# A new written order for TensorE's instructions in a fused attention and gated feed-forward kernel

## The chip, the cores and the metric

The kernel runs on one core of one Trainium2 chip. The metric is device time in microseconds (us). It is the median of several runs; beside it stands one profiled execution with its trace. A core has TensorE (PE, matrix products; PEld is its weight load), VectorE (DVE), ScalarE (ACT), GpSimd (POOL) and SyncE (SP), which run side by side and wait for each other by semaphores. TensorE writes into PSUM, a small memory of eight banks, from which VectorE and ScalarE read.

## The reference

The input x has 4 batches of 12,416 tokens with 128 features. Two attention steps go through 32 inducing points, and a gated feed-forward layer of width 1,536 follows. The types are float32 outside; the kernel computes in float16 with float32 sums.

```python
def mab(q, kv):                       # softmax attention, kv is key and value
    s = scale * (q @ kv.transpose(0, 2, 1))
    s = s - s.max(-1, keepdims=True)
    a = np.exp(s)
    a /= a.sum(-1, keepdims=True) + 1e-09
    return a @ kv
h = mab(I, x)                         # I: the 32 inducing points; h: 32 x 128 per batch
y = mab(x, h)                         # 12,416 x 128 per batch
gate = 1.0 / (1.0 + np.exp(-(y @ w_gate)))
out = (gate * (y @ w_val)) @ w_out    # width 1,536 in between
```

## The kernel before

**Stages.** The first attention (stage 1: h from x) of batch 0 is a prologue of about 30 us. The second attention's weights (stage 2) and the feed-forward layer then run as one long main stretch, in which stage 1 of the next batch is worked in. Since y = a2 @ h, the kernel multiplies h with both feed-forward weights once per batch (`hw`), so the hidden layer is a product of the 32 attention weights a2 with `hw`: a matrix product whose contraction is only 32 long.

**Blocks and chunks.** The tokens lie in 97 blocks of 512 (4 columns of 128). The hidden width of 1,536 is cut in 12 slices of 128. A *chunk* is one slice for one block: a 128 x 512 tile of the hidden layer. Nine chunks of the last batch are worked out apart, by ScalarE and GpSimd (`plan_aside`, L1194); 1,155 remain, in one row. For each chunk there are four kinds of work:

- *Gate*: TensorE multiplies `hw`'s gate part by a2 (32*128 form, L1120, `g_ps`), then ScalarE takes a tanh (L1163) into a ring of 16 chunks in SBUF (`t`). Gates go in units of 2 and 1 chunks in turn, each with a PSUM tile of its own.
- *Value*: TensorE multiplies `hw`'s value part by a2 (same form, same line 1120) into one of two places in PSUM: `v_ps` (two banks) or `vm_ps` (two banks, of which the second also serves the side tasks below).
- *Product*: VectorE forms u = (t + 1) * v (L1350) in one instruction, for one chunk (512 wide) or for two (1024 wide). This is nearly all that VectorE does in the main stretch.
- *Output*: TensorE multiplies u by w_out, four matmuls of the full 128*128 form a chunk (L1249, `acc_ps`). When a block's 48 are done, ScalarE evacuates the sum (L1274) and SyncE writes it out.

The 32*128 form uses a quarter of the array's rows. Row group 0 or 1 is a gate's, for an even or an odd slice, 2 or 3 a value's, and matmuls on different row groups run side by side. TensorE runs them in the order in which they are written.

**Products in pairs.** Products come in first and second ones by turns. A first product reads `v_ps` and takes two chunks. A second one reads `vm_ps`: one chunk (a `V` pair) or two (a `W` pair, only possible while no side task holds the second bank of `vm_ps`).

**Side tasks.** Stage 1 and stage 2 of later blocks and batches are chains of steps over TensorE, ScalarE, VectorE, GpSimd and the DMA queues (`plan_stage1`, `plan_stage2`, `plan_combine`, `plan_aside`). Each has a position, a chunk number from which it may be taken (`TIMES`, `ASIDE`); `turn_page` (L1305) looks for them at every first product. GpSimd's and the DMA steps are issued at once; those of TensorE, VectorE and ScalarE lie in lists until the written order calls them. The loads of x and its transposes are issued by `turn_page` too, at given chunk numbers.

**The written order.** `ORDER`, a string of letters at the top, says in which order instructions are issued; the last loop (L1400) carries it out letter by letter:

- `g`: the next gate unit (`issue_gate`, L1155): its matmuls and its tanh.
- `V` or `W`: the next value fill (`fill_value`, L1322). Of two in a row that form a pair, the first letter says whether the second product has one chunk (`V`) or two (`W`).
- `x`: the product of the fill before it (`product`, L1337).
- `oN`: the next N output matmuls, from a queue to which each product adds four a chunk.
- `p`, `a`, `d`: the next TensorE, ScalarE or VectorE step of a side task.

So a letter's place sets the order on every engine. Between engines nothing is fixed: each waits by semaphores for what it reads and for the buffers that it writes. The product's results have four buffers each for first and second products (L137). A wide product has a no-op ahead of it that waits for its tanhs.

Of the kernel before, what the change touches and what calls it, by code (L numbers as in the profile page):

```python
# [59 lines left out]
4Vxo4go8Vxa0go4pgVxo4pa0gWxo8gVxo8Wxgo8a0gVxgo16gVxgpVxpo4a0gWxo4Vxgo8go4gVxo8gVxo4pa0gVd0xa0gVx  # L60
o20gWxo4Vxgo8go4gVxo8pVxo4Vxa0gpVxgo12Vxa0ggVxo12gVxgo4gVxo4pgVd0xVxo4go12Vxa0a0ggVxo12Vxa0gpgVd
0xo12Vxgo8a0gVxo4VxgpVd0xgo12a0gVxgpVxo8pa0gVxo4pVxgpo4a0gWxo12gVxo4gVxo8gpVd0xgo8a1a0gWxgo8Vxo4
Wxgo8go4gVxo8gVxo8gpVxgpVxa0go8Vxa0gVxo4Vxgpgo8Vd0xVxgo24Vxa0ggVxo12a0gVxpa0gVxo12gVxo4pa0gVxo4p
gVxo12a0gVxo4gVxo4pgVxo8pa0a0gVd0xgVxo12pa0gWxo4gVxo8ggWxo8gVxo8gWxo8a1gVxgo8Vxgo8pVxgo4pVxa1go8
a0gVxo8gWxo8gVxo4a0gWxgo12Vxgo4gWxo8gVxgo8Vxgo8gVxo8a0gVxgo4Vxo8Vxa0go12gVxgVxo4Vxgpo4gVd0xo4gVd
0xo12Vxa0gpo4pVxa0go4gWxo4Vxgo8go4gWxo8gVxo8Vxgo8a0gpa0gVxo8Wxgo8gVxo8Wxgo4Vxgo4ggWxo8gVxo8a0gWx
go8gVxo8gWxo12Vxa0ggo8gVxo8po4a0a0gVxgWxo12Vxgo4Wxgo8gVxgo8gWxo8gVxo8a0ggWxo8gVxo8gVxo4go4pVxpa0
gWxgo12Vxgo8Wxgo4a0gVxgo8gWxo8gVxo8gWxo4go4gVxo8gWxo8a0gVxgo12Wxa0go4Vxgo8gWxo4ggVxo8gWxo12a0gVx
go12Wxgo4gVxo8gWxgo8gVxo4go12Vxa0gpVxgo4pVxa0go8Vxgo8Wxgo4Vxgo8gVxo4go4pVd0xgo8Vxa1a0go12Vxgo4Wx
go4Vxgo8Wxggo4Vxgo16Vxa0gVxgo8pVd0xgo16Vxa0gVxgppVxa0go8Wxgo4Vxgo12a0gWxgo4Vxgo8Vxa0go12ppa0gVxo  # L70
4Wxgo4gVxo8gWxo8a0gVxgo8Vxgo12pgVxo4pa0gVxo4Vxgo12gVxo8a0gVxpVd0xgo12a0gVxo4gWxo4Vxgo4go8Vxgo4Vx
go8Vxgo4a0gVxpVd0xgo4a0gVxo16WxggVxo12gVxgo8pVxgo4pVxo4a0a0gVxgo4Vxa0go12pVd0xgVxo12a0gVxgpo4Vd0
xo4Vxgo12Vxa0gpo4pa0gVxo4gVxpo4pVxa0go4gWxo8Vxgo8ggVxo4Vxgo4pVd0xgo8a1a0gVxgo8Wxo8Vxgo4Wxgo4ggVx
o12gVxo12Vxa0gpgo8Vd0xVxgo8a0go8Vxgo4pVxgo8Vxa0go4Vxgo8Vxa0gppVxa0go8Vxa0go4pVxpa0gWxgo12Vxgo8gV
# [24 lines left out]
o8a0gVxo4gVxpo8a0gVxo4gVxo16Vxa0gVxgo16gVxpa0gVxo16gVxo8Vxgo8Vxa0gVxgo12Vxgo4Vxgo8gVxo8Vxgo4gVxo
4Vxgo8a0gVxgo8VxgVxo4gVxo12VxpVxa0go12gVxgVxo8gVxo4a0gVxgo12VxVxo20Vxo16  # L100
"""


# [1339 lines left out]
```

## Time and profile before

| what | value |
| --- | --- |
| median of 3 runs | 726.4 us (724.94 to 727.75) |
| profiled execution, its own time | 723.66 us |
| its span, first to last instruction | 721.9 us |
| mean granted TensorE clock | 0.996 |
| busy: PE, DVE, ACT, POOL | 684.1, 701.4, 679.2, 445.9 us |
| the prologue, 0 to 30.6 us: DVE busy | 20.33 us |
| the main stretch, 50 to 710 us: PE, DVE, ACT busy | 632.90, 655.10, 640.67 us |

Rows of groups give line, engine, operation, what is written and read with shapes, count, then busy time and mean duration of one in ns, then the idle time ahead of them and what ended it. Rows of the timeline give start, duration, engine, line, operation and count, with the idle time ahead in brackets; several like instructions in a row are one row. Rows of waits give who waited for whom, the sum in us, how often, and the longest. Matmuls overlap and their ends are modelled, so TensorE's busy time says little of how full it is; starts are surer than ends.

### The profile page before, as it was taken

The page shows a single profiled execution, that of the slowest core. Times are in us where ns is not written, and L with a number is a line of the kernel's source. Part 1 is how long each engine was busy: PE and PEld are TensorE (multiplying, and loading weights), DVE is VectorE, ACT ScalarE, POOL GpSimd, SP SyncE. Part 2 cuts the span into 40 slices and gives each one's busy share as a digit, 9 for nine tenths or more (in the row PEclk, how much of TensorE's full clock was granted, in tenths as well). Part 3 has the DMA queues.
Part 4 walks back from the last instruction along what each step waited for, and adds up shares of the span by engine and source line. Part 5 has one row for each costly group of instructions (what it writes and reads, how often), then busy time and mean ns, then how long its engine had stood idle before and what let it go on. Part 6 is the DMA issues. An engine that isn't in the chain of part 4 may idle for free.

```text
span 721.9 us, 21194 instructions
## 1 busy us (share of the span) xinstructions
PE 684.1 (95%) x8446; PEld 401.4 (56%) x8446; DVE 701.4 (97%) x763; ACT 679.2 (94%) x1019; POOL 445.9 (62%) x718
## 2 busy tenths in 40 slices
PE   8899999999999999999999999999999999999997
PEld 4455555555555555555555555555555555555555
DVE  6899999999999999999999999999999999999997
ACT  4699999999999999999999999999999999999996
POOL 4464762888753747488666266378766768776220
PEclk9999999999999999999999999999999999999999
DMA  9799494244458273326178431321220221223111
GB/s 210 119 175 138 107 172 103 60 104 103 91 114 162 66 135 76 74 64 130 49 114 170 102 78 38 89 59 45 62 75 36 69 75 45 61 74 61 45 45 46
DMA packets 118179, 65.74 MB, mean 91 GB/s; under 512 B 101408, under 2 KB 102208, under 8 KB 118080
## 3 DMA queue, kind: packets, MB, share of 16 engines
q1 hardware_dynamic: 112176, 50.90, 30.7%
q0 software_dynamic: 5584, 13.34, 11.0%
q8 instruction: 66, 1.08, 0.6%
q14 instruction: 33, 0.27, 0.1%
q10 hardware_dynamic: 320, 0.15, 0.1%
HBM read 27.80 MB, written 25.43 MB: 74 GB/s over the span
## 4 chain that ended last, share of the span: by engine, by line
PE 52%; ACT 23%; DVE 10%; issue 9%; POOL 3%; DMA 2%; ACTq 0%; DVEq 0%; POOLq 0%
PE acc_ps L1249 25%; ACT t L1163 18%; PE g_ps L1120 13%; DVE u L1350 10%; PE v_ps L1120 5%; PE vm_ps L1120 4%; ACT o L1274 3%; DMA xn<-in_x_dram 2%; PE vm_ps L650 1%; PE vm_ps L427 1%; DMA a2r<-a2n 1%; ACT e L711 1%; ACT a1T L392 1%; POOL a2n L765 1%; PE vm_ps L367 0%
## 5 line engine op out<-in xcount | busy, mean ns | idle before, releaser
L1163 ACT ACTIVATE t<-g_ps 128x1024 f16<-128x1024 f32 (+1 forms) x770 | 588.4, 820 | 19.2 <-ACT t L1163 4.1
L1350 DVE SCALAR_TENSOR_TENSOR u<-t,v_ps 128x1024 f16<-128x1024 f16 (+1 forms) x332 | 401.4, 1209 | 4.1 <-PE v_ps L1120 1.2
L1249 PE MATMUL acc_ps<-wo,u 128*128 128x128 f16 x4596 | 364.2, 220 | 6.6 <-ACT o L1274 1.1
L1249 PEld LDWEIGHTS <-u 128*128 128x128 f16 x4620 | 265.2, 98 | 152.7 <-issue 145.1
L1350 DVE SCALAR_TENSOR_TENSOR u<-t,vm_ps 128x512 f16<-128x512 f16 (+1 forms) x330 | 311.9, 945 | 2.4 <-PE vm_ps L1120 0.9
L1120 PE MATMUL g_ps<-a2r,hwt 32*128 32x512 f16 (+1 forms) x1179 | 287.9, 375 | 13.8 <-ACT t L1163 6.9
L1120 PEld LDWEIGHTS <-hwt 32*128 32x128 f16 x2382 | 97.1, 91 | 128.2 <-issue 55.9
L1120 PE MATMUL v_ps<-a2r,hwt 32*128 32x512 f16 (+1 forms) x677 | 127.2, 374 | 6.4 <-DVE u L1350 4.6
L1120 PE MATMUL vm_ps<-a2r,hwt 32*128 32x512 f16 (+1 forms) x502 | 126.3, 377 | 1.2 <-DVE u L1350 0.9
L719 POOL TENSOR_TENSOR sum<-e 128x256 f32<-128x256 f16 (+1 forms) x23 | 15.4, 671 | 122.3 <-ACT e L711 119.4
L765 POOL TENSOR_TENSOR a2n<-e,rs 128x2048 f16<-128x2048 f16 (+3 forms) x25 | 86.8, 3474 | 3.7 <-DVE rs L737 1.9
L743 POOL TENSOR_TENSOR near<-sme,minus 128x16 f32<-128x16 f32 (+1 forms) x22 | 65.3, 2966 | 1.7
L1274 ACT ACTIVATE o<-acc_ps 128x512 f32<-128x512 f32 x96 | 57.9, 603 | 0.8 <-PE acc_ps L1249 0.4
L698 POOL TENSOR_SCALAR rise<-rise 128x256 f32<-128x256 f32 (+6 forms) x110 | 51.2, 465 | 9.7
L697 POOL TENSOR_TENSOR rise<-sc 128x256 f32<-128x256 f32 (+1 forms) x22 | 16.2, 739 | 32.6 <-ACT sc L687 32.5
L699 POOL TENSOR_TENSOR top<-top,rise 128x128 f32<-128x128 f32 (+3 forms) x88 | 28.4, 323 | 7.3
L719 POOL TENSOR_TENSOR sum<-sum 128x128 f32<-128x128 f32 (+3 forms) x92 | 28.4, 309 | 7.2
L697 POOL TENSOR_TENSOR rise<-top 128x128 f32<-128x128 f32 (+3 forms) x88 | 27.3, 310 | 6.9
L1214 POOL TENSOR_SCALAR xn_spare<-xn_spare 128x512 f32<-128x512 f16 x9 | 13.4, 1492 | 19.9 <-ACT xn_spare L1212 19.9
L702 POOL TENSOR_TENSOR sc<-sc,top 128x512 f32<-128x512 f32 (+1 forms) x22 | 23.9, 1086 | 1.7
L1219 POOL TENSOR_TENSOR xn_spare<-xn_spare 128x512 f16<-128x512 f32 x9 | 11.4, 1272 | 21.2 <-ACT xn_spare L1217 21.1
L650 PEld LDWEIGHTS <-xT 128*128 128x128 f16 x388 | 14.0, 96 | 7.2 <-issue 6.8
(165 smaller groups left out, 330.9 us busy)
## 6 DMA issues: line engine op xcount, KB each, us to landing
out_dram<-o SPq DMA_DIRECT2D x96, 256.0 KB, 2.1
xn<-in_x_dram POOLq DMA_DIRECT2D x18, 512.0 KB, 6.6
xn<-in_x_dram POOLq DMA_DIRECT2D x3, 544.0 KB, 8.2
xn<-in_x_dram POOLq DMA_DIRECT2D x3, 256.0 KB, 12.6
xn<-in_x_dram SPq DMA_DIRECT2D x1, 576.0 KB, 5.6
xn<-in_x_dram SPq DMA_DIRECT2D x1, 512.0 KB, 4.7
a2r<-a2n SPq DMA_TRANSPOSE x29, 4.4
wg<-in_moe_w_gate_dram POOLq DMA_DIRECT2D x1, 384.0 KB, 12.7
```

What stands on the lines that cost most here:

```text
L697: nc.gpsimd.tensor_tensor(out=r, in0=far, in1=near, op=ALU.subtract)
L698: nc.gpsimd.tensor_scalar_max(out=r, in0=r, scalar1=0.0)
L699: nc.gpsimd.tensor_tensor(out=top[:, 0:n, 0:w], in0=near, in1=r, op=ALU.add)
L702: nc.gpsimd.tensor_tensor(out=sc[:, 0:n, :], in0=sc[:, 0:n, :], in1=top[:, 0:n, 0:1].to_broadcast((P, n, m)), op=ALU.subtract,)
L719: nc.gpsimd.tensor_tensor(out=d[:, 0:n, :], in0=src[:, :, 0:w], in1=src[:, :, w : 2 * w], op=ALU.add)
L743: nc.gpsimd.tensor_tensor(out=near[:, 0:n], in0=sme[:, 0:n], in1=minus1[:, 0:n], op=ALU.pow)
L765: eng.tensor_tensor(out=a2n[:, 0:n, :, :], in0=e.unsqueeze(2).to_broadcast((P, n, 4, m)), in1=rs.unsqueeze(2).unsqueeze(3).to_broadcast((P ...
L1120: made_mm.append(nc.tensor.matmul(out[:, col : col + nb * P], hw[b][r : r + 32, j // 2, :], a2r[r : r + 32, o : o + nb, :].rearrange("p j ...
L1163: i = nc.scalar.activation(out=ring[:, p : p + n, :], in_=g[:, 0:n, :], func=AF.Tanh, scale=0.5)
L1249: mm = nc.tensor.matmul(acc[0][half][:, i, :], u[:, ts(i, P)], wo16[:, j, :], start=(i in fresh), stop=not left[ib] and not any(e[1] == ib ...
L1274: nc.scalar.mul(out=o32[:], in_=bank_[:], mul=0.5)
L1350: x = nc.vector.scalar_tensor_tensor(out=u[:, 0:n, a:e], in0=ring[:, p : p + n, a:e], scalar=1.0, in1=v[:, 0:n, a:e], op0=ALU.add, op1=ALU ...
```

## The change

Only `ORDER` is different: TensorE's written order is drawn up anew by a planner outside the kernel, one that reckons with longer changes of form, sets a price on TensorE's pauses and searches more widely. All functions, buffers, positions of the side tasks and sizes of the gate units are as before. The diff is 43 lines of letters out and 43 in; its first and last lines:

```diff
@@ -55,49 +55,49 @@
 ORDER = """
-ggVxggVxpVxgVxo4ggVxgVxpo12gVd0xo8go4gVxo4Vxgo4a0gVxo8Wxo4a0gVxgo12gWxo4gVxo12gVxgo8pgVxpo4a0gWx
-o8a0gVxVxgo12gpVd0xgo4a0gWxo16gVxo4go4Wxgo8a0gVxVxgo12gpVd0xgo4a0gWxo12gVxo4gWxo4go8Vxgo4a0gWxgo
...
-4Vxgo8a0gVxgo8VxgVxo4gVxo12VxpVxa0go12gVxgVxo8gVxo4a0gVxgo12VxVxo20Vxo16
+ggVxgVxgpVxgo8VxgpgVxo12Vd0xgo4ggVxo8Vxa0go4gWxo12Vxa0ggWxo12Vxgo4go4Vxgo4gVxo8Vxgppa0gVxo4Wxgo1
+2Vxa0gVxgo12gpVd0xgo4a0gVxo4Vxgo12gWxo4Vxgo8gVxo4a0gpVd0xgo16a0gWxo8gVxo4gWxo8gVxgo12a0gVxgVxo12
...
+8gVxo4Vxgo12Vxa0gpa0gVxo20gVxVxpa0go12Vxgo8gVxo8Vxa0gVxgo12VxgpVxa0go12Vxgo8gVxo4VxgVxgo12a0gVxg
+Vxo12VxggVxo12gVxo4gVxo8gVxo4gVxo8a0gVxgVxo8gVxpa0gVxo12gVxo4Vxgo12gVxo4Vxgo8a0gVxgVxo16VxVxo32
 """
```

Counted over the whole strings:

| | before | after |
| --- | --- | --- |
| gate units `g` | 770 | 770 |
| products `x` | 661 | 676 |
| pairs: second product 1024 wide (`W`) | 164 | 141 |
| pairs: second product 512 wide (`V`) | 166 | 197 |
| runs of output matmuls `o` (4,656 matmuls in all) | 620 | 608 |
| side steps `p`, `a`, `d` | 140, 214, 34 | 140, 214, 34 |

In the old order the last chunk is a first product by itself, cut in two pieces; in the new one it is the last of the 197 second products, cut in the same way.

More of the change, by code (lines that the diff above doesn't have):

```diff
@@ L63 @@
[L63 to L74, printed above, removed]
@@ L99 @@
[L99 to L100 removed]
+ggVxgVxgpVxgo8VxgpgVxo12Vd0xgo4ggVxo8Vxa0go4gWxo12Vxa0ggWxo12Vxgo4go4Vxgo4gVxo8Vxgppa0gVxo4Wxgo1
+2Vxa0gVxgo12gpVd0xgo4a0gVxo4Vxgo12gWxo4Vxgo8gVxo4a0gpVd0xgo16a0gWxo8gVxo4gWxo8gVxgo12a0gVxgVxo12
+Vxa0gpgVxpo8a0gWxo4gVxo4go4gVxo4Vxgo12Vxa0ggVxo12gVxo4pgVxpo4a0gVxo12Vxgo4gVxo4gVxo8pa0gVd0xa0gV
+xo16gWxo4gVxo4ggVxo8pgVxgpVxo4a0gVxo12a0gVxgVxpo8gVd0xo4Vxgo16a0gWxgo8gVxo12a0gVxgpVd0xo4a0gVxo4
@@ new lines @@
+pa0gVd0xo12gVxpo4pVxgo8a0gWxo4gVxo12a0ggWxo12Vxgo4gVxo8gpVxpa0gWxo8gVxo16Vxa0ggpVd0xgo8a0gWxo8Vx
+go8gVxo8gpVxgpVxa0go8Vxgo4Vxo4Vxa0ggpo12gVd0xo8a0gVxo8gVxpo4a0gVxo8Vxgo8pa0gVxpa0gWxo8gVxo4Vxgo1
+2pa0gVxo4pa0gWxo4gVxo16a0ggVd0xo4po4a0gVxo4Wxgo8gVxo4gWxo8go4gVxo4Wxgo8a1gVxgo12gVxo4pgVxpo4a1gV
+xo8Vxa0go4gVxo8gVxo8Vxa0ggVxo12Wxgo4Vxgo4gVxgo8Vxgo4gVxo4gVxo12Vxa0gVxgo12gVxo4a0gVxo12Vxgo4Vxgp
+o4Vd0xgo4gVd0xgo8Vxpa0gVxpo4a0gWxo8gVxo8gWxo4gVxgo12gVxo12pa0a0gVxgo4Wxo8gVxo4gWxgo12gVxo8Wxgo4g
+Vxo8a0gWxgo12Vxgo4go4a0gWxo12gVxo16a0gVxVxgpo8a0gWxo8gVxo4go4Wxgo4gVxo8gWxgo12a0gVxgWxo12gVxo8go
@@ new lines @@
+4gVxo4pgVxpo4a0gWxo4Vxgo12a0ggWxo8Vxgo4gWxo8Vxgo8go4gWxo8Vxgo8a0gWxgo12gVxo12Wxa0ggVxo8go4Wxgo12
+a0gVxWxgo8go4Vxgo8Wxgo4go4Vxgo4Wxgo8gVxo8a0ggVxo8pVxgpo4a0gWxo12gVxo4gWxo4ggVxo8gVxo8Vxa0gpgo8Vd
+0xgo12Vxa0go4Wxgo8Vxgo4Vxgo4gpVd0xo8Vxa1a0ggo4Vxo8gWxo4Vxgo12gVxgo4ppa0gVxo4Wxgo12a0gVxVxgo16pa0
+gVxo4gVxpa0gVxo12gWxo8gVxo8a0gWxgo12Vxgo4gVxo8gpVxpa0gWxo4gVxo4go4gVxo4Vxgo8pa0gVd0xa0gVxo20gWxo
+4Vxgo4go8gVxo4gVxo8a0gVxpgVd0xo16a0gWxgo4Vxo8Vxggo4pgVxo4pVxa0ggVxo12Vxa0gpVd0xgo16Vxa1a0go4gVxo
+8po4Vd0xgo8Vxgo4VxgpVxo4pa0a0gWxgo12gVxo8gVxo8pgVxo4pVxa0go4gVxo8gVxo4Vxpa0ggVd0xo8a0gVxo16gWxo4
@@ new lines @@
+Vxgo4go8gVxo4gVxpo4Vd0xa0gVxo4a0go12gVxpa0gVxo12gVxpgVxpo8a0gWxgVxo12a0gWxgo12gVxo12Vxa0ggo8pVxp
+Vxa0go4Vxgo12a0gVd0xgVxpo12a0gWxo8Vxgo4go4gWxo4Vxgo8gWxo8a1ggVxo8gVxo8pVxgpo4a1gVxo8a0gVxo4gVxo4
+gVxo12Wxa0ggVxo12Wxgo4go8gVxo4gVxo4ggVxo8Vxgo4Vxo4a0gVxgo12gVxo4Vxa0go8gVxo4VxgVxgo4pVd0xgo4Vd0x
+go12Vxa0gpVxpo8a0gWxgo8gVxo8gVxo8pVxa0go4gWxo4gVxo8a0ggWxo16gVxo8Wxgo4ggVxo8gWxo8gVxo4a0ggWxo12g
+Vxo8gWxo8a0gVxgo20Vxa0ggpVxo8a0gWxo12Vxgo4gWxo8go4gVxo4gWxo8a0gVxgo12gVxo4pgVxpo4a0gWxo8gVxo8gWx
+o8gVxo4a0ggWxo12gVxgo8gWxo4gVxo4gWxgo8Vxggo12Wxa0gVxgo20Wxa0go4gVxo8ggWxo4Vxgo8gWxo4a0ggVxo16gWx
@@ new lines @@
+o8gVxo4ggVxo8gVxo12Vxa0gpgVxo4po4a0gWxo8gVxo8gWxo4ggVxo8gVxo12Vxa0gpgo8Vd0xgVxo4a0go8Wxgo4Vxgo8g
+Vxo4gVxgpo12Vd0xVxa0ga0go16Vxgo8Vxo4VxgppVxa0go8gWxo4gVxo8a0gWxgo8Vxgo16Vxa0go4pgVxpo4a0gWxo4Vxg
+o12a0ggWxo12Vxgo8gVxo4gpVxpa0gWxo4gVxgo8gVxo4gVxo8pa0gVd0xa0gVxo20gWxo4gVxo4go8gVxo4gVxpo8a0gVd0
+xVxgo16a0gVxgo4Vxo8VxgpVxgo8pVxa0ggVxo12a0gVxpVd0xgo16Vxa1a0go8VxgpgVd0xo4gVxo12gVxpVxgpo8a0a0gW
+xgVxo12gVxo4gpVxpa0gWxgo12gVxo8gVxo4Vxgo8pa0gVd0xa0gVxo20gWxo4gVxo4go8gVxo4gVxo8a0gVxpVd0xgo4gVx
+o12Vxa0go12gVxpa0gVxo12VxgpgVxo8pa0a0gVxgVxo12Vxgo4pa0gVxpo4a0gVxo8gVxo8gVd0xo12pVxa0a0ggWxo12gV
@@ new lines @@
+xo4gWxo4gVxo12Vxa0ggo8gVxo8a0gVxgVxo12gVxpo4pa0gVxo4Wxgo4Vxgo8gWxgo8gVxgWxo8a0gVxgo12gVxo4Vxgpo8
+gVd0xo4Vd0xgo8gWxgo12Vxa0gVxgo16a0gVxo8gWxo8Vxgo8gWxo8a0gVxgo12gVxo4pgVxpa0gVxgVxo12gVxpa0gVxo8W
+xgo12Vxa0gWxgo12gVxo4go4Wxgo8gVxo8gWxgo8Vxgo4a0gWxgo12Vxgo8Wxgo8a0gVxgo20a0gVxVxo4pa0gWxgo8gVxo8
+gWxo4go4gVxo4Wxgo8gVxo8a0ggVxo8pgVxo4pa0gWxo12gVxo4gWxo8gVxgo4Wxgo8a0ggVxo12gWxo4Vxgo8gWxgo12gVx
+o8gWxo4a0ggVxo20Vxa0go4pa0gVxo8Wxgo12gVxo4a0gWxgo4Vxo4go4gWxo8gVxo8gWxo4go4gVxo12a0gVxgo4pVxpo4a
+0gWxo8Vxgo4go4gVxo4pa0gVxo8gWxo12a0gVxWxgo12Vxgo4go8gVxo4pa0gVxo8Wxgo12Vxa0gWxgo8Vxgo4go8gWxo4a0
```

34 lines of the change are left out of this document (7 added, 27 removed).

## The prediction

> **What bounds the kernel now.** I read the page first: the busy shares and the chain that ended last.
>
> ```profile
> span 721.9 us, 21194 instructions
> PE 684.1 (95%) x8446; PEld 401.4 (56%) x8446; DVE 701.4 (97%) x763; ACT 679.2 (94%) x1019; POOL 445.9 (62%) x718
> PE 52%; ACT 23%; DVE 10%; issue 9%; POOL 3%; DMA 2%; ACTq 0%; DVEq 0%; POOLq 0%
> ```
>
> Three engines stand at 94 to 97%, and the chain names PE (TensorE) most. That does not settle it: the chain steps back through whoever released the last wait, and in a ring of buffers that is often TensorE even where another engine sets the pace. So I turned to VectorE's (DVE's) own groups in the main stretch (by shape, 30.6 to 717.6 us), and to its timeline, for the time from one start to the next, which busy times do not give.
>
> ```profile
> L1350 DVE SCALAR_TENSOR_TENSOR u<-t,v_ps 128x1024 f16<-128x1024 f16 x330 | 400.6, 1214 | 4.1 <-PE v_ps L1120 1.2 <-PE g_ps L1120 0.6 <-ACT t L1163 0.3
> L1350 DVE SCALAR_TENSOR_TENSOR u<-t,vm_ps 128x1024 f16<-128x1024 f16 x164 | 199.1, 1214 | 0.9 <-PE vm_ps L1120 0.5
> L1350 DVE SCALAR_TENSOR_TENSOR u<-t,vm_ps 128x512 f16<-128x512 f16 x166 | 112.8, 679 | 1.5 <-ACT t L1163 0.5 <-PE vm_ps L1120 0.4 <-issue 0.2
> L379 DVE TENSOR_REDUCE nm<-vm_ps 128x1 f32<-128x512 f32 x18 | 12.3, 682 | 0.0
> ```
>
> ```profile
> 30.68 1.22 DVE L1350 SCALAR_TENSOR_TENSOR u<-t,v_ps 128x1024 f16<-128x1024 f16 x1 [0.27 <-ACT t L1163]
> ...
> 300.93 0.68 DVE L1350 SCALAR_TENSOR_TENSOR u<-t,vm_ps 128x512 f16<-128x512 f16 x1
> 301.53 1.21 DVE L1350 SCALAR_TENSOR_TENSOR u<-t,v_ps 128x1024 f16<-128x1024 f16 x1
> 302.66 1.21 DVE L1350 SCALAR_TENSOR_TENSOR u<-t,vm_ps 128x1024 f16<-128x1024 f16 x1
> 303.79 1.21 DVE L1350 SCALAR_TENSOR_TENSOR u<-t,v_ps 128x1024 f16<-128x1024 f16 x1
> ...
> 716.89 0.75 DVE L1350 SCALAR_TENSOR_TENSOR u<-t,v_ps 128x384 f16<-128x384 f16 x2
> ```
>
> A product starts about 0.08 us before the one ahead ends (301.53 against 300.93 + 0.68). Start to start a wide product therefore takes 1.13 us (302.66 to 303.79) and a narrow one 0.60 (300.93 to 301.53). From the first product's start at 30.68 to the last piece's end at 717.64 (716.89 + 0.75) are 686.96 us. In them VectorE needs (330 + 164) x 1.13 = 558.2, 166 x 0.60 = 99.6, 0.75 for the two last pieces, 18 maxima of 0.60 = 10.8, and some 3 us (estimate) for a dozen small instructions: 672.4. So VectorE works at 98% of what it could, and **about 14 us** are stalls, most of them too short to show as idle. VectorE is the bound; anything that does not lower its work or these 14 us changes nothing.
>
> The other engines have more room:
>
> ```profile
> 50.00:710.00 660.00, 632.90 (x7788) 371.38 (x7786) 655.10 (x669) 640.67 (x951) 419.05 (x669) 1.00 0.40 86
> ```
>
> ```profile
> DVE u L1350 <- PE v_ps L1120: 1.2, 4, 0.4
> DVE u L1350 <- PE vm_ps L1120: 0.9, 2, 0.5
> DVE u L1350 <- ACT t L1163: 0.8, 2, 0.5
> DVE u L1350 <- PE g_ps L1120: 0.6, 3, 0.2
> ...
> PE g_ps L1120 <- ACT t L1163: 7.1, 29, 0.5
> PE v_ps L1120 <- DVE u L1350: 4.6, 13, 0.7
> ```
>
> The first row (one long window; PE, PEld, DVE, ACT, POOL) shows VectorE idle for 4.9 us of 660, ScalarE (ACT) for 19. The waits of VectorE that show come to 3.5 us, of which TensorE's matmuls end 2.7 (1.2 + 0.9 + 0.6) and tanhs 0.8. I carry that ratio over to all 14 us: some 10.8 by TensorE being late, 3.2 by ScalarE. TensorE itself pauses 11.7 us for a tanh or a product that has not yet been read: it is early there, and late elsewhere. An order can mend that.
>
> **What the change does, counted in its letters and priced from rows.**
>
> *VectorE's work.* The new order has 338 first products (all wide) and 338 second ones (141 wide, 197 narrow, the last of these cut in two pieces as before). Against 494 wide and 166 narrow ones before, these are 479 and 196: 15 x 1.13 = 16.95 us go, 30 x 0.60 = 18.0 come. **+1.05 us**, on the engine that is the bound, hidden by nothing.
>
> [...]
>
> *TensorE's work.* Its timeline prices a stretch of order:
>
> ```profile
> 304.05 0.39 PE L1120 MATMUL vm_ps<-a2r,hwt 32*128 32x512 f16 x2
> 304.05 0.38 PE L1120 MATMUL g_ps<-a2r,hwt 32*128 32x512 f16 x1
> 304.37 1.29 PE L1249 MATMUL acc_ps<-wo,u 128*128 128x128 f16 x20
> 305.59 0.39 PE L1120 MATMUL v_ps<-a2r,hwt 32*128 32x512 f16 x2
> 305.60 0.60 PE L1120 MATMUL g_ps<-a2r,hwt 32*128 32x512 f16 x3
> 306.13 0.62 PE L1249 MATMUL acc_ps<-wo,u 128*128 128x128 f16 x8
> 306.69 0.39 PE L1120 MATMUL vm_ps<-a2r,hwt 32*128 32x512 f16 x2
> ...
> 46.88 0.36 PE L650 MATMUL vm_ps<-hT,xT 128*128 128x32 f16 x8
> ```
>
> Twenty `o` take 1.22 us (304.37 to 305.59), eight 0.56: 0.055 each and 0.12 for the change of form. A narrow run in which each row group is used once takes 0.32 (304.05 to 304.37); one that uses a group twice, 0.54 (305.59 to 306.13): 0.22 a round and 0.10 for the change. Counted over the letters: runs of `o` 620 before, 608 after; narrow runs (`g`, `V`, `W`) 662 and 660, with 810 and 799 rounds. That saves 11 x 0.22 + 14 x 0.11 = 3.9 us of TensorE. The 140 `p` steps stay; beside narrow runs they stand 189 times for 177, beside `o` 85 for 93; whether a form changes there is not to be read from the letters, so some 1.3 us (12 x 0.11) either way. With 0.4 us for a `p` (above the 0.36 of the last row) TensorE needs about 631 us of the 687 before and 627 after: it is not the bound, and these 3.9 us are worth only what they take out of the stalls.
>
> *The stalls, TensorE's part.* VectorE stalls where TensorE's work between value fills runs ahead of VectorE's for several products on end. I took, for every stretch of 2, 4, 6 and 8 products, TensorE's need minus VectorE's at these prices, and added up what is above zero (divided by the length). Before and after: 39.9 and 33.9 us for two, 19.0 and 15.4 for four, 9.9 and 6.7 for six, 7.0 and 4.1 for eight: 15, 19, 32 and 41% less (with a dearer `p`, 0.55: 12, 17, 21 and 27%). The new order is the more even one, though not by far. The bounds are nothing and 41% of 10.8 us, thus 0 to -4.4. I take the mean of four and six, 26%, because the two value banks let TensorE be one product ahead at most and its slack against VectorE (0.06 us a product) fills that up in some five: **-2.8 us**. The `o` runs also ask for older products (the youngest asked for is at most two products back in 303 of 608 runs, in 408 of 620 before), so they will wait for VectorE less; I count nothing for that.
>
> *The stalls, ScalarE's part.* Here the new order is the worse. The gate matmul of a product's last chunk stands at most one product ahead of it 108 times, 60 times before (ten times in the very step, twice before). The two waits of VectorE for a tanh above, 0.8 us, came with 60; 48 more would bring 1.6 more waits of 0.4: **+0.6 us**. Bounds: nothing, as ScalarE is idle 19 us, and, if the whole 3.2 us grow with the count, +2.6.
>
> *The ends.* Near the end VectorE stands idle for 0.38 us:
>
> ```profile
> 715.10 1.22 DVE L1350 SCALAR_TENSOR_TENSOR u<-t,v_ps 128x1024 f16<-128x1024 f16 x1 [0.38 <-PE v_ps L1120]
> ...
> 34.00:36.00 2.00, 2.00 (x24) 1.27 (x20) 1.88 (x3) 1.72 (x3) 0.00 (x0) 0.50 0.76 120
> ...
> 37.14 1.22 DVE L1350 SCALAR_TENSOR_TENSOR u<-t,v_ps 128x1024 f16<-128x1024 f16 x1 [0.33 <-PE v_ps L1120]
> 38.73 0.69 DVE L1350 SCALAR_TENSOR_TENSOR u<-t,vm_ps 128x512 f16<-128x512 f16 x1 [0.37 <-PE vm_ps L1120]
> ```
>
> The new end, `VxVxo16VxVxo32` for `VxVxo20Vxo16` in substance, has both last fills ahead of the last `o`s, whose 32 x 0.055 = 1.8 us fit beside the last two products (1.13 + 0.75): **-0.4**. At the start TensorE's granted clock (third column from the right in the row of the window) is 0.50 around 34 to 36 us, and two idle times of 0.70 us together follow. The new start has the same amount of work there; whether the halved stretch comes again I cannot read, so -0.7 to +0.7, counted as nothing.
>
> *Sum:* +1.05 - 2.8 + 0.6 - 0.4 = -1.6 us (rounded). The profiled execution took 723.66 us with a span of 721.9; I expect 722.1 and 720.3. The three runs have a median of 726.4 (724.94 to 727.75), 2.7 above the profiled one; the difference carries over: **724.8 us**. About 0.5%, 3.6 us, is what a measurement of this kernel can tell from no change; -1.6 is below that.
>
> **The rivals.** *The stalls go by half or more.* If most of the 14 us come from single late fills which an evener order removes, 7 to 9 us go: with +1.05, -6 to -8, thus about 719.5. For it: overloads over eight products fall by 41%, and runs of `o` ask for older products. Against: over two products they fall by 15% only, and the tanhs stand closer.
>
> *The tanhs decide (slower).* Each of the 48 further products whose gate stands at most one product ahead waits. A gate must be filled (0.39 us above) and pass ScalarE before its product, and a product ahead gives 0.60 or 1.13 us for it; a step of another kind on ScalarE in between is enough to be late. From 0.14 us a case on it decides: the 1.05 of VectorE's work, less 0.4 and 2.8, and 48 x 0.14 = 6.7 make +4.6, thus 731. For it: the narrow products' idle time in their group above is put down to a tanh first of all (0.5 of 1.5). Against: 60 such cases cost 0.8 us in idle time before, and ScalarE has the room.
>
> *The order does not do what it says.* TensorE's pauses and changes of form come down, and VectorE, which never depended on them, shows only its +1.05 us: 727.4, no change that can be told. The 2.7 of 3.5 us that TensorE ends speak against it. [...]
>
> **How the numbers follow.** The forecast, with all that stays within 3.6 us, 0.40; the order that gains nothing, 0.12, also within; the halved stalls 0.33, beyond 0.5% faster; the tanhs 0.15, slower. So faster 0.33, same 0.52, slower 0.15. The range goes from 718.0 (-8.4: the further end of the halved stalls) to 730.5 (+4.1: just inside the tanh case), which leaves out about a tenth on each side. The forecast's own bounds, 0 to -4.4, 0 to +2.6 and 0.7 at the start, give 721 to 729.
>
> **What would show it.** In the profile after: 479 wide and 196 narrow products at unchanged 1214 and 679 ns, so VectorE busy some 2 us more (durations overlap); its stalls by the same sum near 11.5 instead of 14 us; TensorE's waits for tanhs and products below 11.7 us; VectorE's waits for tanhs about 1.4 instead of 0.8 us. If the stalls are 14 us again while TensorE's work fell, my link from windows of products to stalls is wrong. If they are below 8, single late fills were their cause. If the waits for tanhs exceed 3 us, the third case holds.

## The result, and the profile after

The new order takes **717.35 us** (median of 4 runs, 716.64 to 720.78); before it were 726.05 us (4 runs, 724.94 to 727.75). The ratio is 0.9884, with a 95% interval of 0.9851 to 0.9918: faster by 8.7 us or 1.2%. The forecast was 724.8, the range 718.0 to 730.5: the result lies just below the range, nearest to the rival "the stalls go by half or more" (719.5).

Runs of one kernel differ by how long TensorE was granted half its clock (mean clocks of 0.981 to 1.000 in the runs of before, 0.992 to 1.000 in those of after); "at full clock" below means a mean granted clock of 0.998 or more, which still leaves room for one stretch of 3.4 us at half, as after_again has one below at 0.998. At full clock the kernel before takes 722.1 to 723.3 us, with 722.5 in the middle of nine, the one after 716.6 to 718.6, with 717.1 in the middle of eight. So the order by itself is worth some 5.4 us, and the rest of the 8.7, some 3, goes with less time at half clock. The profiled execution of after (720.78 us, clock 0.992) is the longest of its four runs.

The page of the kernel after: its span, the busy times and the chain.

```profile
span 719.0 us, 21227 instructions
...
PE 689.1 (96%) x8446; PEld 403.3 (56%) x8446; DVE 698.0 (97%) x778; ACT 678.4 (94%) x1019; POOL 445.6 (62%) x718
...
PE 54%; ACT 18%; DVE 13%; issue 7%; DMA 3%; POOL 3%; DVEq 0%; ACTq 0%; POOLq 0%
```

VectorE's busy time has gone down, though it has 15 more instructions. A busy time is the time covered by at least one instruction; products that overlap a little more (0.08 us at 705.40 us in the rows below) cover less. The groups by shape (30.6 to 717.6 us) show the work itself:

```profile
L1350 DVE SCALAR_TENSOR_TENSOR u<-t,v_ps 128x1024 f16<-128x1024 f16 x338 | 409.6, 1212 | 4.4 <-PE v_ps L1120 2.2 <-PE g_ps L1120 1.3
L1350 DVE SCALAR_TENSOR_TENSOR u<-t,vm_ps 128x1024 f16<-128x1024 f16 x141 | 170.9, 1212 | 0.3
L1350 DVE SCALAR_TENSOR_TENSOR u<-t,vm_ps 128x512 f16<-128x512 f16 x196 | 132.9, 678 | 0.9 <-PE vm_ps L1120 0.5 <-ACT o L1274 0.4
```

The three sum to 713.4 us, against 400.6 + 199.1 + 112.8 = 712.5 before. VectorE's timeline gives the times from start to start:

```profile
30.84 1.22 DVE L1350 SCALAR_TENSOR_TENSOR u<-t,v_ps 128x1024 f16<-128x1024 f16 x1
...
704.80 0.68 DVE L1350 SCALAR_TENSOR_TENSOR u<-t,vm_ps 128x512 f16<-128x512 f16 x1
705.40 1.21 DVE L1350 SCALAR_TENSOR_TENSOR u<-t,v_ps 128x1024 f16<-128x1024 f16 x1
706.53 0.68 DVE L1350 SCALAR_TENSOR_TENSOR u<-t,vm_ps 128x512 f16<-128x512 f16 x1
...
713.79 0.74 DVE L1350 SCALAR_TENSOR_TENSOR u<-t,vm_ps 128x384 f16<-128x384 f16 x2
```

A narrow product still takes 0.60 us (704.80 to 705.40) and a wide one 1.13 (705.40 to 706.53). By the prediction's sum VectorE now needs 479 x 1.13 + 196 x 0.60 + 0.74 + 10.8 + 3 = 673.4 us, and it took 713.79 + 0.74 - 30.84 = 683.7. The stalls are **10.3 us**. Before they were 686.96 - 672.4 = 14.6 by the same sum, which the prediction calls about 14. Some of the 10.3 lie in a stretch at half clock, which the profiled execution of before did not have in this place (a clock of 1.00 there from 110 to 126 us). The windows there, with the matmul that waited ahead of the stretch:

```profile
114.00:118.00 4.00, 2.71 (x31) 1.45 (x30) 2.71 (x5) 2.59 (x5) 0.65 (x1) 0.96 0.65 171
118.00:122.00 4.00, 4.00 (x31) 2.17 (x29) 2.89 (x3) 2.87 (x5) 0.00 (x0) 0.50 0.16 33
122.00:126.00 4.00, 4.00 (x65) 2.48 (x62) 2.73 (x4) 2.88 (x4) 0.00 (x0) 0.68 0.00 0
```

```profile
116.05 0.39 PE L1120 MATMUL g_ps<-a2r,hwt 32*128 32x512 f16 x2 [1.28 <-DMA a2r<-a2n]
```

The third column from the right is the granted clock. A mean of 0.96, 0.50 and 0.68 over 4 us each means 0.3, 4.0 and 2.6 us at half, 6.9 us in all. In the 8 us from 118 VectorE is busy for 5.6 (2.89 + 2.73). The stretch goes from 117.7 to 124.5 us, with 0.50 in the shorter windows within it; it begins 1.7 us after the end of a wait of 1.28 us for a transposing DMA (`a2r`, a side task).

The waits (30.6 to 717.6 us) of VectorE and then of TensorE:

```profile
DVE u L1350 <- PE v_ps L1120: 2.2, 5, 0.7
DVE u L1350 <- PE g_ps L1120: 1.3, 3, 0.7
DVE nm L379 <- PE vm_ps L367: 0.9, 1, 0.9
DVE u L1350 <- PE vm_ps L1120: 0.5, 2, 0.4
```

```profile
PE v_ps L1120 <- DVE u L1350: 2.5, 12, 0.2
PE g_ps L1120 <- DMA a2r<-a2n: 2.1, 2, 1.3
PE g_ps L1120 <- ACT t L1163: 2.0, 10, 0.3
PE vm_ps L1120 <- DVE u L1350: 1.8, 9, 0.3
```

This is where the two kernels differ most. TensorE waited 7.1 us in 29 places at a gate, for a tanh that had not yet read the gate's PSUM tile; now it is 2.0 us in 10. Its waits at value fills for a product are 4.3 us in 21 places, 5.5 in 18 before: more, and shorter. VectorE's waits for a tanh, 0.8 us before, no longer show.

### The profile page after: what moved, and what is told of

Read it like the earlier page. It is cut to its first block, busy times and chain, and to the rows that moved or that the text cites. A ratio compares the mean times of both kernels' runs of the same rounds, so it can differ in the third digit from the quotient of the medians.

```text
span 719.0 us, 21227 instructions
## 1 busy us (share of the span) xinstructions
PE 689.1 (96%) x8446; PEld 403.3 (56%) x8446; DVE 698.0 (97%) x778; ACT 678.4 (94%) x1019; POOL 445.6 (62%) x718
## 4 chain that ended last, share of the span: by engine, by line
PE 54%; ACT 18%; DVE 13%; issue 7%; DMA 3%; POOL 3%; DVEq 0%; ACTq 0%; POOLq 0%
PE acc_ps L1249 25%; PE g_ps L1120 15%; ACT t L1163 14%; DVE u L1350 13%; PE v_ps L1120 5%; PE vm_ps L1120 5%; ACT o L1274 2%; DMA xn<-in_x_dram 2%; DMA a2r<-a2n 1%; PE vm_ps L650 1%; PE vm_ps L427 1%; POOL a2n L765 1%; ACT sc L687 1%; ACT a1T L392 0%; POOL near L743 0%
## 5 line engine op out<-in xcount | busy, mean ns | idle before, releaser
L1350 DVE SCALAR_TENSOR_TENSOR u<-t,v_ps 128x1024 f16<-128x1024 f16 x338 | 409.6, 1212 | 4.4 <-PE v_ps L1120 2.2
L1350 DVE SCALAR_TENSOR_TENSOR u<-t,vm_ps 128x512 f16<-128x512 f16 (+1 forms) x339 | 304.6, 899 | 1.3 <-PE vm_ps L1120 0.5
L1120 PEld LDWEIGHTS <-hwt 32*128 32x128 f16 x2382 | 99.0, 91 | 118.9 <-issue 44.0
L1120 PE MATMUL v_ps<-a2r,hwt 32*128 32x512 f16 (+1 forms) x692 | 130.5, 375 | 4.4 <-DVE u L1350 2.5
L1120 PE MATMUL vm_ps<-a2r,hwt 32*128 32x512 f16 (+1 forms) x487 | 129.8, 377 | 2.6 <-DVE u L1350 1.8
L1219 POOL TENSOR_TENSOR xn_spare<-xn_spare 128x512 f16<-128x512 f32 x9 | 11.4, 1272 | 21.7 <-ACT xn_spare L1217 21.5
```

Source lines behind the costliest of these rows:

```text
L1120: made_mm.append(nc.tensor.matmul(out[:, col : col + nb * P], hw[b][r : r + 32, j // 2, :], a2r[r : r + 32, o : o + nb, :].rearrange("p j ...
L1350: x = nc.vector.scalar_tensor_tensor(out=u[:, 0:n, a:e], in0=ring[:, p : p + n, a:e], scalar=1.0, in1=v[:, 0:n, a:e], op0=ALU.add, op1=ALU ...
```

## The experiments

The theories, as the expectations name them. **1:** single late value fills caused the stalls, all along the kernel, and the new order has its fills in time. **2:** the gain is TensorE's smaller work, its fewer changes of form. **3:** a few long stalls and the ends make it up. **A:** the wait for `a2r` sets off the half clock (in after_again alone this is called theory 2). After the first runs two more were set up: **5:** TensorE pauses at gates that are written before ScalarE has emptied their tile, and the fill queued behind each comes late; **6:** the stalls lie in TensorE's own order, whatever ScalarE does.

**after_again.** The kernel after once more, unchanged, beside 19 runs of before.

> The kernel after, unchanged, for a second trace. Theory 1 (the new order writes the value fills so that they come in time, all along the kernel): without the halved TensorE clock that the first trace shows at 117 to 124 us, VectorE's stalls should be 5 to 6 us instead of 9, the span about 715 and the time 716 to 718. Theory 2 (the halved clock belongs to this order, since TensorE waits for the attention weights of the fourth group at 115 us): the stretch at half clock and its 3 us of stalls are there again and the time is near 720.

718.3 us (716.64 to 720.13, six runs), ratio 0.990 (0.9871 to 0.9929). The profiled execution (718.56 us) has the same wait of 1.28 us and then 3.4 us at half clock (means of 0.78 from 114 to 118 us and 0.80 from 118 to 122), half as long as the first time. Its stalls are 8.6 us by the sum above, 1.7 less than in the execution with the longer stretch. So the stretch came back, as the second theory there has it, but the time stayed below 720.

**old_first and new_first.** One order up to chunk 479, the other behind it, in both combinations; the strings are joined where both stand at the same chunk.

```diff
 ORDER = (first half of one, second half of the other)
```

> Old order up to chunk 479, new order from there. Theory 1 (gain spread over the whole): VectorE's stalls behind that place are 8.0 us before and 3.2 after, and 20 of the 23 wide pairs given up lie here (about 0.9 us of VectorE's work): -4 us, thus 722. Together with the opposite half the two gains should add up to the whole. Theory 3: none or all, 726 or 717.

> New order up to chunk 479 (317 us), old order from there, at a place where both have issued the same gates, chunks, output matmuls and side steps. Theory 1 (gain spread over the whole): the part up to there holds 6.8 us of VectorE's stalls before and some 3 after without a halved clock; -3 to -4 us against the kernel before, thus 722 to 723. Theory 3 (a few long stalls or the ends make the gain): all of it or none, 717 or 726.

old_first: 722.91 us (719.42 to 726.98), ratio 0.9964 (0.9938 to 0.999); at full clock 719.4 to 721.0 in four runs, thus by the middles (722.5, 720.2, 717.1) 2.3 us below before and 3.1 above after. The second half of the new order brings less than half of the gain, and by subtraction the first half the rest. That speaks against theory 3. new_first: 730.02 us, ratio 1.0075 (1.0047 to 1.0103), which says nothing of the orders, so that the two gains could not be added up: at the joint a chain of a side task came late once,

```profile
DVE li L516 <- PE vm_ps L602: 5.6, 1, 5.6
```

and a stop of 5.6 us with its half clock behind it (0.88, 0.50 and 0.60 over 5 us each from 320 us; 0.982 to 0.993 over the whole runs) covers what was to be seen.

**turn_early.** The new order; the DMA of the `a2r` that made TensorE wait 1.28 us is issued one position earlier.

```diff
-            (weigh + (5 if soon else 8 if far is None else 7), "do", turn, 0),
+            (weigh + (5 if soon else 8 if far is None else 7) - ((at, c) == (0, groups[3][0])), "do", turn, 0),
```

> The kernel after, with the transposing DMA of the fourth group's attention weights (batch 0) issued one position earlier, so that on SyncE's queue it stands ahead of an output and of a transpose that waits for ScalarE (issued at 110.66 us now, though its input is ready at 105.4). If the queue is what makes it late: TensorE's wait of 1.3 us at 115 us goes, with it the chance of a halved clock behind it; -1 to -1.5 us against the kernel after in undisturbed runs, -3 to -4 against its slowest, and closer runs. If the transfer itself is slow or another takes its place: no change, 717.

**715.57 us** (715.12 to 716.28), ratio 0.9865 (0.9835 to 0.9894), and all six runs with a clock of 0.999 or 1.000. This is the best version, 1.35% below before. The two ends of VectorE's main stretch, and TensorE's waits (50 to 705 us):

```profile
29.92 1.22 DVE L1350 SCALAR_TENSOR_TENSOR u<-t,v_ps 128x1024 f16<-128x1024 f16 x1 [0.27 <-ACT t L1163]
...
708.28 0.75 DVE L1350 SCALAR_TENSOR_TENSOR u<-t,vm_ps 128x384 f16<-128x384 f16 x2
```

```profile
PE v_ps L1120 <- DVE u L1350: 2.1, 10, 0.2
PE vm_ps L1120 <- DVE u L1350: 1.8, 9, 0.3
PE g_ps L1120 <- ACT t L1163: 1.8, 9, 0.3
```

The wait for `a2r` is gone and so is the half clock (1.00 over the whole profiled execution); the stretch is 709.03 - 29.92 = 679.1 us and the stalls are 5.7. With the clock out of the way this is the cleanest picture of the new order: **14.6 us of stalls became 5.7**. The 14.6 have a stretch at half clock in them; at full clock they would be some 13 (an estimate: the profiled execution, 723.66, lies 1.2 above the middle of 722.5).

**before_turn.** The same in the old order (two positions earlier, `- 2 * (...)` in the same line).

> The kernel before, with the transposing DMA of the fourth group's attention weights issued earlier, at the same place on SyncE's queue as in turn_early. Theory A (TensorE's wait for these weights at 115 us is what sets the clock to a half for a while in many runs of the old order too): the median falls from 725.4 to 721.5 to 722.5, where the runs of the kernel before at a granted clock of 1.00 lie, and the spread from 5 us to under 2. Then some 3 us of the 8 us between the two kernels are clock and not order. Rival (the halved clock comes from elsewhere in the old order): 724 to 726 with the same spread.

724.58 us (721.7 to 728.83, 12 runs), ratio 0.9989 (0.9967 to 1.0011): no change. Clocks are 0.983 to 0.998, so theory A does not carry over: in the old order the half clock comes in other places too. In the profiled execution it was here,

```profile
459.00:463.00 4.00, 4.00 (x31) 2.10 (x32) 2.75 (x4) 2.69 (x5) 0.00 (x0) 0.52 0.17 35
463.00:467.00 4.00, 4.00 (x50) 2.35 (x48) 2.51 (x4) 3.14 (x6) 0.00 (x0) 0.62 0.00 0
```

behind waits, between 450 and 459 us, of 0.3 us at a gate and 0.7 us for another `a2r`. At full clock it takes 721.7 and 722.35 us. This kernel is the base of the other edits of the old order below.

**before_turn_mended.** before_turn, with the fills of 51 products that stalled written four to eight output matmuls earlier.

```diff
-...Vxpo12gVd0xo8go4gVxo4Vxgo4a0gVxo8Wx...
+...Vxpo12gVd0xo8ggVxo8Vxgo4a0gVxo4Wxo8...
```

> before_turn, and in its order 51 value fills that stalled VectorE by 0.05 us or more in the trace of before (7.3 us in all) are written four output matmuls earlier (0.22 us; eight for the three longest): the four stand behind the product instead of ahead of the fill. Nothing is added or left out. Theory 1 (the fills' place makes the stalls): up to 6.2 us of these stalls go, -3 to -5 us against before_turn. Theory 2 (TensorE has too much work, and the new order gains by its 3.9 us less): the lateness only moves to the next fill, and the changes of form that it adds (636 runs of output matmuls for 620) cost; 0 to +2.

730.97 us (730.53 to 735.32), ratio 1.0095 (1.0072 to 1.0119); slower by 8 at full clock (730.5 and 730.6). Moving the fill forward moved the gates forward with it, and TensorE's waits at gates went from 6.3 to 11.1 us:

```profile
PE g_ps L1121 <- ACT t L1164: 11.1, 41, 0.6
```

So theory 1 fails in this form: a fill can't simply be written earlier. What stands in its way showed here first, and led to theory 5.

**before_turn_less and before_turn_light.** before_turn, with 72 of the 4,656 output matmuls left out (4.0 us of TensorE at 0.055, as much as the change was to save), and with 416 left out (23 us). Both lines stand at the head of the output matmul; the sums lack these terms.

```diff
+        if ib % 4 != 3 and j == 2 and i == 0 and i not in fresh and left[ib] and not final:
+            return
```

```diff
+        if j % 4 == 3 and i not in fresh and left[ib] and not final:
+            return
```

> before_turn with 72 of the 4,656 output matmuls left out, one in three blocks of four (their share is missing from the output): 3.96 us less for TensorE, as much as the new order saves it, with the old places of the fills. Theory 2 (less work for TensorE is the gain): -5 to -6 us against before_turn. Theory 1 (the places): each left-out matmul moves the fills behind it by 0.055 us only, -0.5 to -1.5.

> before_turn with 416 of the output matmuls left out (those of one hidden slice in most blocks; their share is missing from the output): 23 us less for TensorE. If VectorE is the bound and TensorE's lateness makes most of its stalls: they fall from 13 to between 3 and 7 us, -6 to -10 against before_turn. If the stalls are ScalarE's or the semaphores': -1 at most. A stretch at half clock, should TensorE idle too much, would show in the granted clock.

less: 722.11 us (721.06 to 736.54), ratio 0.996 (0.9943 to 0.9976); at full clock 721.1 to 722.4 in eight runs, between nothing and some 1 us below before_turn's two (721.7 and 722.35). Its median is 2.5 us below that of before_turn, as eight of its ten runs were at full clock and only two of twelve there. light: 725.27 us (722.12 to 731.03), ratio 1.0017 (0.9991 to 1.0043); at full clock 722.12 and 722.13, nothing gained. **Theory 2 fails as the whole cause:** 23 us less work for TensorE, six times what the change saves, and the time stays. TensorE's waits (50 to 705 us) of light show that much of it went into pauses, at gates 11.1 us for 6.3 in before_turn:

```profile
PE g_ps L1120 <- ACT t L1163: 11.1, 44, 0.5
PE v_ps L1120 <- DVE u L1352: 7.4, 21, 0.9
```

**before_swap and before_swapall.** before_turn; a gate that stands ahead of a fill is put behind it, in the 56 places where it waited, and in all 358 where it can be.

```diff
-ggVxggVxpVxgVx...
+ggVxgVgxpVxgVx...
```

```diff
-ggVxggVxpVxgVx...
+gVgxgVgxpVxVgx...
```

> before_turn with 56 pairs of letters gV written Vg: those whose gate's matmul stood waiting in the trace of before for a tanh to free its place (7.3 us of TensorE in all), with the value fill next behind it. Theory 5 (TensorE's pauses: it stands at a gate that was written too early, and the fill queued behind it comes late for VectorE; the pauses also set off the halved clock): 3 us of stalls are behind such a wait in before, so at a full clock 719 instead of 721.7, and the median -3 to -5 against the 724.6 of before_turn. Theory 2 (less work, fewer changes of form) expects nothing: neither changes here.

> before_turn with all 358 pairs gV written Vg, whether the gate waited or not. Theory 5: at least as good as before_swap where the pause was the harm, unless tanhs come late for it: 717 to 722. Rival (the tanh's lateness decides, as each gate now stands a step later): slower than before_turn.

swap: 724.22 us (722.35 to 728.74), ratio 0.9973 (0.9952 to 0.9993); at full clock 722.35 to 722.9 in five runs, no gain. Its waits at gates did fall, from 6.3 to 4.1 us; those at fills rose from 4.5 to 6.3:

```profile
PE v_ps L1120 <- DVE u L1350: 6.3, 20, 0.7
PE g_ps L1120 <- ACT t L1163: 4.1, 17, 0.5
PE vm_ps L1120 <- DVE u L1350: 2.5, 11, 0.4
```

swapall: 731.61 us (727.7 to 736.0), ratio 1.0085 (1.0057 to 1.0114); 727.7 and 727.9 at full clock, with 4.8 us at gates. Both miss what theory 5 expected of them. In swapall the waits at gates are shorter than in before_turn (6.3), and yet it is slower by 5 to 6 us; the waits do not name the mechanism. A gate that is put off also puts off its tanh, but that this is the cause was not tried.

**before_lag.** before_turn with the output matmuls four later within each block.

```diff
-ggVxggVxpVxgVxo4ggVxgVxpo12...
+ggVxggVxpVxgVxggVxgVxpo12...
```

> before_turn with the output matmuls moved four places back within each block: a run asks for products one chunk older, as the new order does (the youngest asked for is at most two products back in 217 of 604 runs; 408 of 620 before, 303 of 608 after). 3.1 us of stalls in before come right behind an output matmul for which TensorE had stood idle. Theory 5: these go, -2 to -4 against before_turn. Rival (gates come earlier for it and wait longer, as in before_turn_mended): no change or slower, with TensorE's waits for tanhs above 8 us.

733.78 us (732.43 to 740.37), ratio 1.0127 (1.0092 to 1.0162), with no run at full clock. With the output matmuls gone from ahead of them the gates come earlier, and wait longer:

```profile
PE g_ps L1120 <- ACT t L1163: 11.0, 36, 0.6
PE v_ps L1120 <- DVE u L1350: 5.2, 17, 0.6
```

**turn_early_gates and turn_early_gates_half.** The test from the other side: turn_early, with 214 gates (and with every other of them, 107) written one step earlier, ahead of the product instead of behind it. Letters and counts, changes of form and fills stay what they are.

```diff
-ggVxgVxgpVxgo8VxgpgVx...
+gggVxgVxpgVxo8gVxpgVx...
```

```diff
-ggVxgVxgpVxgo8VxgpgVx...
+ggVxggVxpVxgo8gVxpgVx...
```

> turn_early (the new order) with 214 gates moved ahead of the value fill in the same narrow run: Vxg written gVx. No change of form is added. Theory 5: gates come before their place is free, TensorE waits for tanhs 5 us or more instead of 1.8, the fills behind are late: 718 to 722 instead of 715.6, with stretches at half clock. Theory 2 (work and changes of form): 715.6 again.

> turn_early with every second of the 214 gates moved ahead of the value fill (107). Theory 5: about half of the loss of turn_early_gates (7.4 us at full clock), 718 to 720.5. If a few bad places made that loss: near 715.6 or near 723.

gates: 724.64 us (722.77 to 728.11, 12 runs), ratio 0.9987 (0.9965 to 1.0009), at full clock 722.8 to 724.1 in five runs: **the whole gain is lost**, more than theory 5 expected (718 to 722). half: 719.47 us (718.66 to 721.66), ratio 0.9916 (0.9884 to 0.9947), at full clock 718.7 to 720.2: half of it. TensorE's waits at gates, first of the full, then of the half edit:

```profile
PE g_ps L1120 <- ACT t L1163: 5.6, 24, 0.5
PE v_ps L1120 <- DVE u L1350: 0.4, 2, 0.2
```

```profile
PE g_ps L1120 <- ACT t L1163: 3.2, 15, 0.3
PE v_ps L1120 <- DVE u L1350: 1.2, 5, 0.4
```

So 0, 107 and 214 gates moved give 1.8, 3.2 and 5.6 us at gates and, by the middle of the runs at full clock, 715.6, 719.4 and 723.0 us. The stalls of VectorE, by the same sum as above, go from 5.7 to 9.9 and 14.2 in the profiled executions; the last two have 3.4 and 6.8 us at half clock in them. One of these waits in the timeline of the full edit:

```profile
192.89 0.61 PE L1249 MATMUL acc_ps<-wo,u 128*128 128x128 f16 x8
193.03 1.22 DVE L1350 SCALAR_TENSOR_TENSOR u<-t,v_ps 128x1024 f16<-128x1024 f16 x1
193.81 0.39 PE L1120 MATMUL g_ps<-a2r,hwt 32*128 32x512 f16 x2 [0.31 <-ACT t L1163]
193.82 0.39 PE L1120 MATMUL vm_ps<-a2r,hwt 32*128 32x512 f16 x2
...
194.28 1.22 DVE L1350 SCALAR_TENSOR_TENSOR u<-t,vm_ps 128x1024 f16<-128x1024 f16 x1
```

TensorE is done with its output matmuls at 193.50 and could fill `vm_ps`. But the gate stands ahead in its queue, and waits 0.31 us for a tanh to free its tile; the fill goes out together with it. The product was due at 193.03 + 1.13 = 194.16 and starts at 194.28. That is 0.12 us of stall, and VectorE's row shows no idle time.

**before_turn_act and turn_early_act.** ScalarE relieved in both orders: the tanh covers 384 of each 512 columns (the rest of the ring is zero), 84 and 88 us less of ScalarE's busy time (50 to 705 us). Theory 5 lets the two orders meet, theory 6 lets their distance stay.

```diff
+    CUT = 384
+    nc.gpsimd.memset(ring[:, :, CUT:], 0.0)
...
-            out=ring[:, p : p + n, :], in_=g[:, 0:n, :], func=AF.Tanh, scale=0.5
+            out=ring[:, p : p + n, 0:CUT], in_=g[:, 0:n, 0:CUT], func=AF.Tanh, scale=0.5
```

> before_turn with each tanh on 384 of its 512 columns (the last quarter of every gate is left out and reads as 0.5): some 120 us less for ScalarE, nothing else changed. Theory 5 (VectorE stalls because TensorE stands at a gate until ScalarE frees its place, or the tanh itself is late): the stalls behind gates (3.1 us) and late tanhs (3.5) go and the half clock with them; 714 to 718 instead of 724.6 (721.7 at full clock). Theory 6 (the stalls are in the order of TensorE's own work, whatever ScalarE does): 720 or more at full clock.

> The same cut of the tanhs in turn_early, the new order. Theory 5: there is little left behind gates (0.3 us) and tanhs (2.1), so 713 to 714.5 instead of 715.6; the 6 us between the orders at full clock shrink to 1 to 3, and with all stalls gone the new order would be the slower by its 1 us of VectorE's work. Theory 6: the 6 us between the orders stay.

The old order: 715.59 us (713.35 to 722.71), ratio 0.9869 (0.9823 to 0.9914); at full clock 713.4 to 714.2 in three runs, some 8 below before_turn. The new one: 714.03 us (713.48 to 714.58), ratio 0.9837 (0.9804 to 0.9869); at full clock 713.5 to 714.1, only some 1.6 below turn_early. **The orders meet.** This relieves both TensorE's waits at gates and any late tanh at once, and does not tell the two apart. TensorE's waits (50 to 705 us), old order first:

```profile
PE v_ps L1123 <- DVE u L1352: 8.6, 28, 0.7
...
PE g_ps L1123 <- ACT t L1165: 0.4, 2, 0.3
```

```profile
PE vm_ps L1123 <- DVE u L1352: 6.5, 27, 0.5
PE v_ps L1123 <- DVE u L1352: 4.9, 22, 0.4
...
PE g_ps L1123 <- ACT t L1165: 0.3, 2, 0.2
```

TensorE still pauses, in the new order for 11.4 us at fills (6.5 + 4.9), about as long as at gates and `v_ps` fills together in before (7.1 + 4.6), but little can be lost by it: VectorE's stalls in this execution are 3.9 us by the sum above. There TensorE waits for VectorE, which is busy (653.9 of 655 us in the new order). At a gate it waits for ScalarE, and VectorE can run dry behind it, as at 194.28 us in turn_early_gates (0.31 us of wait, 0.12 of stall).

**turn_early_light.** The test of theory 2 in the new order: turn_early with 404 output matmuls left out (22 us of TensorE), by the same line as in before_turn_light.

> turn_early with 404 of the output matmuls left out (their share is missing from the output), 22 us less for TensorE, as in before_turn_light. Theory 5: as there, no gain at full clock (715 to 717), more pauses, and half clock in more runs. Theory 2 (TensorE's work): -2 us or more, 713.5 or less.

714.9 us (714.36 to 715.74), ratio 0.9852 (0.9819 to 0.9884); 0.7 us below turn_early. Theory 2 expected more than that, theory 5 a little less (715 to 717). One of its rows limits theory 5:

```profile
PE g_ps L1120 <- ACT t L1163: 5.6, 25, 0.4
```

That is as much waiting at gates as in turn_early_gates (5.6 us in 24 places, 723.0 us), and here it cost nothing; the stalls are 5.0 us. So the sum of the pauses at gates does not set the time by itself. That TensorE, with 22 us less to do, makes up for them in time is the likely reason; no run tried it.

## Why the prediction came out wrong

**What bounds the kernel: right.** VectorE does, and the stalls (14.6 us by the prediction's own sum) were what could be had. What the new order won at full clock came out of them.

**VectorE's work, +1.05 us: it fits the rows, though no run has it alone.** There are 479 wide and 196 narrow products at the same 1.13 and 0.60 us from start to start; two narrow ones thus take 2 x 0.60 - 1.13 = 0.07 us more than a wide one. The check that the prediction named for it, a busy time 2 us higher, was badly chosen: it fell by 3.4 (701.4 to 698.0), as covered time also depends on how closely the products follow each other.

**TensorE's work, 3.9 us less and worth little by itself: right.** Leaving out 4.0 us of it gave between nothing and some 1 at full clock, leaving out 23 nothing in the old order and leaving out 22 0.7 in the new one.

**"The stalls, TensorE's part", -2.8 us: this is the step that failed.** It took the stalls to come from TensorE's work running ahead of VectorE's over several products, and scaled them by 26%. The runs with less TensorE work show that load alone is not their cause. turn_early_gates shows it more plainly: it has the same runs, rounds and changes of form as the new order, and a count over its letters like the prediction's, over 2 to 8 products, stays within some 1%; yet it is 7.4 us slower. So the measure of the step, windows of products, does not see what carries this difference. From 14.6 to 5.7 us of stalls (turn_early) the term was worth -8.9 us, some -8 at full clock, not -2.8.

What the runs show in its place is the order of gates and fills in one queue, against ScalarE's pace. A gate that is written before ScalarE has emptied its tile stops TensorE, and the fill behind it comes late (0.31 us of wait at 193.81 us in turn_early_gates, and a product 0.12 us late). The prediction had the row (7.1 us in 29 waits at gates) and wrote "it is early there, and late elsewhere. An order can mend that", but gave it no term in the sum. Writing 214 gates a step earlier takes 7.4 us back, and with the tanhs a quarter shorter the two orders meet.

That this is the whole of the 8 us is not shown. I followed each product that started 0.03 us or more late from its fill back along TensorE's timeline, to the last pause of 0.04 us or more, as far as 1.5 us ahead of the product before it. Before: 2.5 us of stalls behind a pause at a gate, 2.8 behind a pause ahead of an output matmul, 2.4 where the fill was done in time, 5.4 with TensorE busy all along. In turn_early: 0.3, 0.1, 1.9 and 2.9; with the 214 gates moved: 5.9, 0.1, 1.9 and 5.2. These are estimates and hang on the limits: if only pauses of 0.15 us count, 0.7 us are behind gates before. So pauses at gates account for only 2 to 3 of the 8 us by this reading. As much may be the second item, which the prediction saw ("the `o` runs also ask for older products") and counted at nothing; no run isolates it.

**"The stalls, ScalarE's part", +0.6 us: wrong in sign.** It counted gates that stand close ahead of their product (108 against 60) and feared late tanhs. VectorE's waits for tanhs went to none from 0.8 us. One reading, not tried by a run, is that the count measured the wrong distance, from gate to product and not from gate to the tanh that frees its tile.

**The ends, -0.4, and the start, 0: about right.** Of the 0.38 us near the end 0.18 are left; the first product starts at 30.84 us for 30.68.

**"The difference carries over" (2.7 us from the profiled execution to the median): wrong.** That difference is in the main time at half clock, and the new order has less of it: some 3 of the 8.7 us. For the kernel after, the profiled execution lies 3.4 us above the median, not 2.7 below. It went unread in the prediction, although the mean clock of 0.996 stood in the table.

**The rivals.** The one that came nearest was given 0.33. Its 6 to 8 us less fit the 8.7 partly by luck: some 3 of these are time at half clock, of which it says nothing, and 5.4 are the order. Its check, stalls below 8, is met by turn_early (5.7), not by the profiled executions of after (10.3) and after_again (8.6). Its mechanism, "single late fills", is half right: the fills were late singly, but at least in part because of what stands ahead of them. The tanhs did not make it slower, and VectorE did depend on TensorE's pauses, as the one of 0.31 us in turn_early_gates shows.

**What stays open.** Why repairs of the old order do not pay: swap lowers the waits at gates by 2.2 us and gains nothing, swapall loses 5 us without longer waits at gates. Nor is it simply how far the gates stand ahead: by a count over the letters a gate is written on average 5.0 chunks ahead of the fills before, 4.7 after, 5.0 and 5.2 with 107 and 214 gates moved, which goes with the times, but 4.9 in swap and 4.2 in swapall, which does not. And where the old order's half clock begins, apart from the place at 459 us.

## What to carry to other kernels

Price a pause of an engine that works in written order by what is queued behind it, not by its length or by the engine's load alone: 214 gates one step too early cost 7.4 us of 715.6, while 11 us of pauses at the fills cost nothing that shows, and 5.6 us of pauses at gates cost nothing where 22 us of the work behind them were gone. Look for the places where an engine waits for a resource that another one frees, and test the cause from both sides, by spoiling the good order and by relieving the engine waited for. Writing the waiting instruction later is not a cure by itself: in the old order it gained nothing in 56 places and lost 5 us in 358. And read the granted clock beside each time: it goes with some 3 of the 8.7 us here.

## What the runs showed of the hardware

The granted clock of TensorE fell to half behind short pauses. In after and in after_again it fell within 1.7 us after the end of a pause of 1.28 us, once for 6.9 us (means of 0.96, 0.50 and 0.68 over 4 us each) and once for 3.4 us (0.78 and 0.80); with that pause gone (turn_early) six of six runs had at least 0.999. TensorE was busy for 2.71 of the 4 us around the first pause. A pause of 0.89 us in the same place in the profiled execution of before left the clock at 1.00, but in before_turn pauses of 0.3 and 0.7 us, both between 450 and 459 us, were followed by 6.9 us at half (0.52 and 0.62 over 4 us each). What sets the clock to half and what ends such a stretch, these runs do not show.

The price can be estimated from before alone (its runs beside turn_early_act). A mean clock of 0.991 over 727 us means about 13 us at half; that run took 727.3 us, one with 1.00 on the same chip 722.5. So 13 us at half cost 4.8, some 1.3 us for each 3.4 by this estimate, less than the 1.7 by which TensorE's own clock falls behind in them.
